# One more chunk turned by TensorE instead of by DMA in a fused retention and gated feed-forward kernel, with the state copies, the loads' lead and two casts moved along with it

## The chip, the cores and the metric

The kernel runs on one core of one Trainium2 chip. A core has a matrix engine (TensorE, PE in the profile, with its weight loads as PEld), a vector engine (VectorE, DVE), a scalar engine (ScalarE, ACT), a general engine (GpSimd, POOL) and a sync engine (SyncE, SP), which here issues nearly all DMA transfers. Each engine works through its own queue in order; semaphores tie the queues together. The metric is the device time of one execution in microseconds (us), the median of several runs.

## The reference

First comes a retention layer: attention without a softmax, with a decay per head. For 8 batches, 8 heads, 576 positions and a head dimension of 64:

```python
scores = scale * np.matmul(q, k.transpose(0, 1, 3, 2))
gamma = 1.0 - 2.0 ** (-5.0 - np.arange(H))
Dmat = np.where(rel >= 0, gamma[:, None, None] ** rel[None, :, :], 0.0)   # rel = i - j
attn_out = np.matmul(scores * Dmat, v)
```

Its result, laid out as 4608 tokens of 512 numbers, is `x` for a gated layer with 1536 hidden units:

```python
gate = 1.0 / (1.0 + np.exp(-(x @ w_gate)))
out = (gate * (x @ w_val)) @ w_out
```

## The kernel before

**Chunks.** The decay is folded into q and k by two tables of powers, one for each position in a chunk. Retention then runs over chunks of 128 positions: scores inside a chunk, masked to a triangle, times v, plus q times a running state, the sum of all earlier k-v products of the batch. Batch 0's first 512 positions and batch 1's first 256 are done at the start, in pairs. The other 30 chunks are the list `STEPS`, numbered from 0: 0 and 1 are the end of batch 1, 2 to 5 the four full chunks of batch 2, 6 is the 64 last positions of batches 0 and 1 together, 7 to 10 the full chunks of batch 3, 11 the last positions of batches 2 and 3, and so on.

**What a chunk passes through.** SP loads its k, q and v (`load`, L163, or in halves L166 for a chunk of last positions). `casts_to` has k and q multiplied by their tables and rounded to bf16 (`cast_qk`, L398: on POOL, q of the first two chunks on DVE), has v cast (`cast_v`, L403), and from chunk 2 on calls `cross` (L407): a DMA transpose on SP's queue that turns k and q so that the head dimension lies on the partitions. Chunks 0 and 1 are turned on TensorE instead, by `turn_step`: eight transposing matmuls (L589) into the two PSUM banks `pv` and `tr`, which ACT and DVE copy to SBUF (L591). The turned copy, tile T, is read by the scores (`scores`, L628) and by the products of q with the state (`inter`, L670). The same two banks later hold the chunk's values (`intra`, L654).

`casts_to(x)` also sets the loads' lead: before chunk x's casts it queues the loads up to chunk x + 1, from chunk 12 on up to x + 2. `next_slot(s)` does the scores of chunk s and the values of chunk s - 1, then calls `casts_to(s + 3)`; `next_two` does two chunks at once. Both put what is left over (copies of values, state sums, their bf16 copies) into a list `pending`, of which one entry is taken after each later unit of work.

**The feed-forward layer.** Its tokens go in blocks: 512 tokens at the start, then `BLOCKS`: 256 tokens from row 512 (number 0), 256 from row 768 (number 1), and seven of 512 from row 1024 on (2 to 8). Blocks 0 and 1 are plain: 12 units of hidden products (`h_units`, L847: gates to ACT's sigmoid, L850, values to DVE's product, L852) and 6 units of output products (`op_units`, L1174). Blocks of 512 use a scheme of seven products instead of eight, for which sums of quarters of the weights, of x and of the hidden units are made. The order of their units is written out by hand (`ORDER`): `g16` is product 6 of the gates' second third, `w07` product 7 of the first third of the values, `v8` a plain value product. In `ORDER`, marks behind a colon place sums of the hidden units on DVE or POOL (L902 and L908, tile gsum), which the output products (L1072) read. POOL also does some of the gate-times-value products of these blocks (L989).

**Order around the change.** The main loop over `BLOCKS` goes unit by unit. After each unit it may emit a sum of weights that is due (`weight_sums`, L312 and L338), the in-place sums that `PLACES` puts after that unit, in block 2 the casts that `CASTS_AT` puts there, one pending entry, or the next slot. Blocks 0 and 1 hold four and two slots (chunks 0 to 3, 4 and 5), and block 1 also the first double slot: after its second output unit come the values of chunk 5 and the scores of chunks 6 and 7. Values of later chunks follow in block 2.

`first_batch_state` assembles the state that the last positions of batch 0 (chunk 6) need, in a tile `sf`, by two DVE copies and two small DMAs on SP's queue (L796); it is called in slot 3.

Of the kernel before, what the change touches and what calls it, by code (L numbers as in the profile page):

```python
# [16 lines left out]
def kernel(  # L17
# [139 lines left out]
    def load(s):  # L157
        b, c = STEPS[s]
        tiles = []
        for nm, src in (("k", k), ("q", q), ("v", v)):  # L160
            t = landing([P, H, D], f"{nm}32_{s}", s >= 8)
            if c < LAST:
                nc.sync.dma_start(out=t, in_=src[b, :, c * P:(c + 1) * P, :].rearrange("h p d -> p h d"))  # L163
            else:
                for j, (bj, tj) in enumerate(pieces_of(s)):
                    nc.sync.dma_start(out=t[half(j)], in_=src[bj, :, tj:tj + 64, :].rearrange("h p d -> p h d"))  # L166
            tiles.append(t)
        loaded[s] = tiles
# [137 lines left out]
    def wo_sums(i, part, parts, eng=nc.vector):  # L306

        fp = slice(part * (NFC // 2) // parts, (part + 1) * (NFC // 2) // parts)
        b11, b12, b21, b22 = (wo_sb[:, r::2, c:c + DM // 2][:, fp] for r in range(2) for c in (0, DM // 2))
        t1, t2, t4 = (wt_sb[:, j, fp] for j in range(3))  # L310
        to, a, b = ((t1, b12, b11), (t2, b22, t1), (b12, b22, b12), (t4, b21, t2))[i]
        eng.tensor_tensor(out=to, in0=a, in1=b, op=ALU.subtract)  # L312
# [80 lines left out]
    def cast_qk(s, i, eng):  # L393
        c = STEPS[s][1]
        if i == 1:
            natural_qk[s] = nat_pool.tile([P, 2, M, P], BF16, tag="qk", name=f"qk_{s}")
        tab = (qtab, ktab)[i][:, c, :].rearrange("p (y m) -> p y m", y=2).unsqueeze(3).to_broadcast([P, 2, M, D])
        eng.tensor_tensor(out=natural_qk[s][:, i].rearrange("p m (y d) -> p y m d", y=2),  # L398
                          in0=by_halves(loaded[s][1 - i]), in1=tab, op=ALU.mult)

    def cast_v(s, eng):
        natural["v", s] = nat_pool.tile([P, H, D], BF16, tag="v", name=f"v_{s}", bufs=6)
        eng(out=natural["v", s], in_=loaded[s][2])  # L403

    def cross(s):
        t = att_pool.tile([P, 2, M, P], BF16, tag="T", name=f"T_{s}", bufs=6)
        nc.sync.dma_start_transpose(out=t.rearrange("p j m t -> p (j m) t"),  # L407
                                    in_=natural_qk[s].rearrange("p j m d -> p (j m d)"))
        turned[s] = t
# [168 lines left out]
            cols = slice(t0, t0 + P)  # L578
            eng(out=x_out(slice(i * k, (i + 1) * k), cols), in_=x_in(ps[:, at_m:at_m + k], cols))

    TURNED = 2

    def turn_step(s):

        t = att_pool.tile([P, 2, M, P], BF16, tag="T", name=f"T_{s}", bufs=6)
        for i, ((pool, tag), eng) in enumerate(zip(VALS, (on_act, on_dve))):
            ps = pool.tile([P, M, P], BF16, tag=tag, name=f"turn_{s}_{i}")
            for m in range(M):
                nc.tensor.matmul(ps[:, m, :], lhsT=natural_qk[s][:, i, m, :], rhs=ident, is_transpose=True,  # L589
                                 start=(m == 0), stop=(m == M - 1))  # L590
            eng(out=t[:, i], in_=ps)  # L591
        turned[s] = t
# [81 lines left out]
    def slot(s):  # L674

        if s > 0:
            val_ps[s - 1] = values(M + 2, s - 1)
            intra(s - 1)
            inter(s - 1, [(0, 1), (0, 1)], apart=True)
        scores(s)  # L680
        if STEPS[s][1] < LAST:
            products(s)
        mask(s)
# [84 lines left out]
    def after(s, i):  # L768

        makes = STEPS[s][1] < LAST  # L770
        to_bf16 = on_act if s < 6 else on_pool
        if i == 0:
            if s > 0:
                leave_share(s - 1, 0)
                leave_share(s - 1, 1)
            if makes:
                add_state(s, 0)
        else:
            if s > 0:
                leave_other(s - 1, i - 1)  # L780
                leave_own(s - 1, 2 - i)
                if i == 2 and dealt(cols_of(s - 1, 0)):
                    x_sums(at_col[s - 1], nc.vector)
            if i == 1 and makes:
                add_state(s, 1)
            if makes and (s, i - 1) in totals:
                b, c = STEPS[s]
                keep_state((b, c, i - 1), totals.pop((s, i - 1)), to_bf16)


    def first_batch_state():

        whole = new_state((0, LAST - 1, NJ - 1))
        for hh in range(2):
            for y in range(2):
                (nc.vector.tensor_copy if hh == y else nc.sync.dma_start)(  # L796
                    out=whole[half(y), hh::2, :], in_=sbd[3][half(hh), 2 * y:2 * y + 2, half(hh)])
        state[0, LAST - 1, NJ - 1] = whole

    pending = []  # L800

    done = {"ld": 0, "cast": 0}

    def loads_to(s):
        while done["ld"] <= min(NS - 1, s):
            load(done["ld"])
            done["ld"] += 1

    def casts_to(s):
        while done["cast"] <= min(NS - 1, s):  # L810
            x = done["cast"]
            loads_to(x + (1 if x < 12 else 2))
            cast_qk(x, 1, nc.gpsimd)
            cast_qk(x, 0, nc.vector if x < 2 else nc.gpsimd)
            if x >= TURNED:
                cross(x)
            cast_v(x, on_dve if x == 0 else on_pool)
            done["cast"] += 1

    def next_slot(s):  # L820
        slot(s)
        if s == 3:
            first_batch_state()
        casts_to(s + LEAD_CAST)
        for i in range(3):
            pending.append(lambda i=i: after(s, i))
        if s + 1 == 1:
            pending.insert(2, lambda: turn_step(s + 1))
# [98 lines left out]
    def quarter_units(gvs, t0):  # L927
# [82 lines left out]
        def value(fc):  # L1010
# [3 lines left out]
            for kc in range(NKC):  # L1014
# [6 lines left out]
        return quarter, value  # L1021

    EARLY = ((10, "g01"), (13, "g05"), (13, "g02"))
    PLACES = (((1, 0), "g", 0), ((1, 1), "g", 1), ((1, 2), "w", 0), ((2, 0), "o", 0), ((2, 1), "w", 1),
              ((2, 9), "o", 1), ((2, 12), "g", 2), ((2, 45), "o", 2))
    CASTS_AT = (5, 32)
    SECOND = 7
    ORDER = ("g06 g11 w05 g03 w01 g15 g16 g12 g07 w06 g13 g21 g17 w03 w11 w07 g04 w02 g14 w04 w16:0t"
             " g26:00 w12 w15:01 w17:02 g25 g22 w13 g27 g23 w14:10 v8 v9:1t:2a g24 v10:11 v11:12:2b").split()
# [420 lines left out]
    SPARE = {}  # L1450
    for at, kind, u in PLACES:
        SPARE.setdefault(at, []).append((lambda u=u: wo_sums(2, u, 3)) if kind == "o" else (lambda kind=kind, u=u: w_sums(kind, 2, u, nc.vector)))
# [4 lines left out]
    for w, (t0, n) in enumerate(BLOCKS):  # L1457
        nxt = BLOCKS[w + 1] if w + 1 < len(BLOCKS) else None
        last = last_step(nxt[0] + nxt[1]) if nxt else NS - 1
        end = slots + (SINGLE[w] if w < len(SINGLE) else 0)  # L1460
        begin = slots
        total = 2 * NFC * 4 * n + 12 * 512 * (n // P)
        n_h = NFC if n <= 256 else 2 * NFC
        if n == 512:
            n_h = len(steps_of(t0))
        n_twos = 0
        gone = 0
        twos = []
        at = end
        while not twos and valued + (end - begin) < last or twos and twos[-1][0][-1] < last:  # L1470
            vals = list(range((twos[-1][0][-1] if twos else valued + end - begin) + 1, at))
            twos.append((vals, list(range(at, min(at + 2, NS)))))
            at = min(at + 2, NS)
        if w < 1:
            twos = []

        for i, cols in enumerate(ffn_units(t0, n, nxt)):
            if w < 2 and i % 2 == 1 and weight_sums:
                weight_sums.pop(0)()
            if w == 2 and i in CASTS_AT:  # L1480
                casts_to(done["cast"])
            for x in SPARE.get((w, i - n_h if w == 1 else i), ()):
                x()
            gone += cols
            pieces += 1
            if stores and (nxt is None or w + 2 == len(BLOCKS) and pieces % 4 == 0):
                leave()
            if n > 256 and i % 2 and i < n_h:
                continue
            if pending:  # L1490
                pending.pop(0)()
            elif slots < end and gone * (end - begin) >= (slots - begin) * (total - 5 * 2048):
                next_slot(slots)
                valued = slots - 1
                slots += 1
            elif twos and i - n_h >= (SECOND if n == 512 and len(twos) == 1 else 1):
                next_two(*twos[0], n == 512, not n_twos, len(twos) == 1)
                n_twos += 1
                valued = twos[0][0][-1]
                slots = max([slots] + [s + 1 for s in twos.pop(0)[1]])  # L1500
        assert not twos and slots >= end
        while pending:
            pending.pop(0)()
# [31 lines left out]
```

## Time and profile before

| | |
|---|---|
| timed runs, median (lowest to highest of 3) | 314.72 us (313.76 to 315.41) |
| the profiled execution, whole | 312.58 us |
| its span, first to last instruction | 310.9 us |
| mean granted clock of TensorE | 0.994 |
| busy: PE / DVE / POOL / ACT | 300.3 / 232.8 / 202.5 / 193.6 us |
| moved by DMA | 55.24 MB, mean 178 GB/s |
| DMA transposes | 28, of 2.7 to 6.0 us from issue to landing, median 3.9 |
| the double slot in block 1 | from 84.67 us |
| the first block of 512 from row 1024 | from 93.02 us |

Times inside the execution are counted from the start of the span. A line of a timeline gives the start, the time taken, the engine, the line of the kernel, the operation and its tiles (written <- read), shapes, a count, and in brackets the idle time before it with what ended that. In a group of waits the figures are the sum, the count and the longest, in us. The slices of the page are 40 equal parts of the span, a digit for each: the busy share in tenths, or for PEclk the granted clock in tenths of full speed.

### The profile page before, as it was taken

To read this page: it belongs to the slowest core of one execution; us is meant where nothing else is said; L and a number is where in the kernel's file an instruction comes from. 1 tells how busy PE (TensorE), PEld (TensorE's weight loads), DVE (VectorE), ACT (ScalarE), POOL (GpSimd) and SP (SyncE) were. 2 spreads that over 40 slices of the span, in tenths; PEclk is the share of its full clock that TensorE was granted. 3 is DMA by queue.
4 is the path that set the end of the run, shared out by engine and by line. 5 is a ranking of instruction groups with operands and counts; after the bars stand their busy time and mean duration, and the time that the engine had idled before them with its cause. 6 is when DMAs were issued, how large, how long until landed. Compare 5 with 4: busy or idle time off the path is not lost. (4 is left out here: it accounts for less than half of the span.)

```text
span 310.9 us, 10391 instructions
## 1 busy us (share of the span) xinstructions
PE 300.3 (97%) x4262; PEld 236.2 (76%) x4278; DVE 232.8 (75%) x492; ACT 193.6 (62%) x424; POOL 202.5 (65%) x240
## 2 busy tenths in 40 slices
PE   8999999999979999999999999999999999999994
PEld 7664456868738878887888788878887888788773
DVE  6857967886874997699769876987699769835943
ACT  6855454545329736973797379736973797359730
POOL 6784555643743799878787877797779707810780
PEclk9999999999979999999999999999999999999999
DMA  7999999997999658995479659957981183003004
GB/s 217 345 373 392 350 271 237 223 177 171 203 208 223 149 124 155 247 249 147 112 170 249 156 130 191 243 120 128 183 207 65 36 271 104 2 21 118 3 1 136
DMA packets 146048, 55.24 MB, mean 178 GB/s; under 512 B 125392, under 2 KB 137936, under 8 KB 146000
## 3 DMA queue, kind: packets, MB, share of 16 engines
q1 hardware_dynamic: 145200, 53.92, 71.1%
q8 instruction: 33, 0.54, 0.7%
q10 hardware_dynamic: 800, 0.66, 0.7%
q14 instruction: 15, 0.12, 0.1%
HBM read 37.75 MB, written 9.44 MB: 152 GB/s over the span
## 5 line engine op out<-in xcount | busy, mean ns | idle before, releaser
L398 POOL TENSOR_TENSOR qk<-k,ktab 128x512 bf16<-128x512 f32 x30 | 32.2, 1073 | 22.7 <-DMA k<-in_k_dram 18.7
L966 PEld LDWEIGHTS <-wg_sb 128*128 128x128 bf16 x336 | 32.9, 98 | 5.5
L989 POOL TENSOR_TENSOR gv<-gv,wu 128x512 bf16<-128x512 bf16 x14 | 16.3, 1165 | 29.8 <-DVE wu L1001 29.8
L1072 PEld LDWEIGHTS <-gsum 128*128 128x128 bf16 x336 | 32.3, 98 | 4.3 <-POOL gsum L908 0.4
L398 POOL TENSOR_TENSOR qk<-q,qtab 128x512 bf16<-128x512 f32 x28 | 30.8, 1100 | 1.5 <-DMA q<-in_q_dram 1.5
L902 POOL TENSOR_TENSOR gsum<-gv 128x512 bf16<-128x512 bf16 (+1 forms) x28 | 27.0, 965 | 5.6 <-DVE gv L989 4.7
L966 PEld LDWEIGHTS <-wgt_sb 128*128 128x128 bf16 x252 | 24.6, 98 | 3.3
L643 DVE TENSOR_TENSOR pt<-row,tri 128x256 bf16<-128x256 f32 x60 | 21.6, 416 | 6.6 <-PE row L636 5.0
L1072 PEld LDWEIGHTS <-gv 128*128 128x128 bf16 x240 | 23.0, 98 | 4.3
L1015 PE MATMUL h<-xT,wv_sb 128*128 128x512 bf16 x105 | 24.9, 379 | 0.4
L966 PE MATMUL gatea<-xsum,wg_sb 128*128 128x256 bf16 x168 | 25.2, 273 | 0.0
L1001 DVE TENSOR_TENSOR gu<-gatee,gu 128x512 f32<-128x512 f32 x21 | 14.4, 688 | 12.6 <-ACT gateg L993 6.3
L966 PEld LDWEIGHTS <-wv_sb 128*128 128x128 bf16 x224 | 21.9, 98 | 2.5
L989 POOL TENSOR_TENSOR gv<-gv,ws 128x512 bf16<-128x512 bf16 x14 | 17.1, 1221 | 7.6 <-DVE ws L1004 7.6
L1004 DVE TENSOR_TENSOR gs<-gatea,gs 128x512 f32<-128x512 f32 x21 | 14.4, 688 | 10.1 <-PE gatea L966 9.3
L712 ACT CAST xT<-val 128x256 bf16<-128x256 f32 x50 | 15.7, 386 | 9.1 <-PE val L670 6.0
L403 POOL CAST v<-v 128x512 bf16<-128x512 f32 x29 | 19.4, 670 | 1.4 <-DMA v<-in_v_dram 1.4
L1018 DVE TENSOR_TENSOR gv<-gv,h 128x512 bf16<-128x512 bf16 x28 | 18.4, 679 | 2.4 <-PE h L1015 2.4
L1015 PEld LDWEIGHTS <-wv_sb 128*128 128x128 bf16 x112 | 11.0, 98 | 10.2
L987 ACT ACTIVATE gv<-gs 128x512 bf16<-128x512 f32 x21 | 13.4, 639 | 7.6 <-DVE gs L1004 7.6
L966 PEld LDWEIGHTS <-wvt 128*128 128x128 bf16 x168 | 16.4, 98 | 2.2 <-issue 0.3
L604 ACT CAST sb<-s 128x256 bf16<-128x256 f32 x46 | 17.4, 420 | 1.1 <-DVE s L763 0.2
(178 smaller groups left out, 826.4 us busy)
## 6 DMA issues: line engine op xcount, KB each, us to landing
k<-in_k_dram SPq DMA_DIRECT2D x26, 256.0 KB, 3.8
q<-in_q_dram SPq DMA_DIRECT2D x26, 256.0 KB, 4.3
v<-in_v_dram SPq DMA_DIRECT2D x26, 256.0 KB, 4.7
out_dram<-ob SPq DMA_DIRECT2D x25, 256.0 KB, 3.0
wg<-in_moe_w_gate_dram SPq DMA_DIRECT2D x12, 256.0 KB, 5.3
wv<-in_moe_w_val_dram SPq DMA_DIRECT2D x12, 256.0 KB, 5.2
wo<-in_moe_w_out_dram SPq DMA_DIRECT2D x12, 256.0 KB, 5.0
v32p<-in_v_dram SPq DMA_DIRECT2D x6, 256.0 KB, 4.9
```

What stands on the lines that cost most here:

```text
L398: eng.tensor_tensor(out=natural_qk[s][:, i].rearrange("p m (y d) -> p y m d", y=2), in0=by_halves(loaded[s][1 - i]), in1=tab, op=ALU.mult)
L403: eng(out=natural["v", s], in_=loaded[s][2])
L604: eng(out=state[key], in_=src)
L643: nc.vector.tensor_tensor(out=probs[s][:, y], in0=row_ps[s][y][:, 0], in1=tri.unsqueeze(1).to_broadcast([P, M, 64]), op=ALU.mult)
L712: nc.scalar.copy(out=x_out(ALL, cols_of(s, i)), in_=x_in(val_ps[s][i], cols_of(s, i)))
L902: nc.gpsimd.tensor_tensor(out=s3, in0=a11, in1=a21, op=ALU.subtract)
L966: nc.tensor.matmul(ps[:, f], lhsT=w[:, kc, f * P:(f + 1) * P], rhs=x[:, kc], start=(first and f == 0 and kc == 0), stop=(f == 1 and kc == ...
L989: eng.tensor_tensor(out=to, in0=to, in1=src, op=ALU.mult)
L1001: nc.vector.tensor_tensor(out=me["u2"], in0=e, in1=me["u2"], op=ALU.add)
L1015: nc.tensor.matmul(ps, lhsT=wv_sb[:, kc, fc * P:(fc + 1) * P], rhs=xT(kc, slice(t0, t0 + 512)), start=(kc == 0), stop=(kc == NKC - 1))
L1018: nc.vector.tensor_tensor(out=gvs[fc], in0=gvs[fc], in1=ps, op=ALU.mult)
L1072: nc.tensor.matmul(ps[:, b], lhsT=left(fp)[:, b * P:(b + 1) * P], rhs=right(fp), start=(first and fp == 0 and b == 0), stop=(fp == NFC // ...
```

## The change

Six edits:

- `TURNED` becomes the set of chunks that TensorE turns: 0, 1 and now 7. Chunk 7's DMA transpose is no longer issued.
- `turn_step(7)` is emitted in block 1 after its last hidden unit (`n_h + TURN_AT` is 11) and so ahead of its first output unit.
- `first_batch_state` is called in slot 1 instead of slot 3.
- The loads' lead is given by chunk in `AHEAD`: 2 for chunk 0, 1 for chunks 1 to 8, 2 for chunk 9, 1 for chunk 10, 0 for chunk 11, and 2 as before from chunk 12 on. Before, it was 1 for all chunks up to 11.
- The casts of chunks 10 and 11 in block 2 are emitted after units 2 and 12 instead of 5 and 32.
- The eight in-place sums of weights in `PLACES` stand in other places: two in block 1 (units 12 and 15) instead of three, and six in block 2 (units 0, 6, 7, 10, 17, 43) instead of five (0, 1, 9, 12, 45).

```diff
-    TURNED = 2
+    TURNED = (0, 1, 7)
...
+    AHEAD = (2, 1, 1, 1, 1, 1, 1, 1, 1, 2, 1, 0)
...
-            loads_to(x + (1 if x < 12 else 2))
+            loads_to(x + (AHEAD[x] if x < len(AHEAD) else 2))
             cast_qk(x, 1, nc.gpsimd)
             cast_qk(x, 0, nc.vector if x < 2 else nc.gpsimd)
-            if x >= TURNED:
+            if x not in TURNED:
                 cross(x)
...
-        if s == 3:
+        if s == 1:
             first_batch_state()
...
-    PLACES = (((1, 0), "g", 0), ((1, 1), "g", 1), ((1, 2), "w", 0), ((2, 0), "o", 0), ((2, 1), "w", 1),
-              ((2, 9), "o", 1), ((2, 12), "g", 2), ((2, 45), "o", 2))
-    CASTS_AT = (5, 32)
+    PLACES = (((1, 0), "w", 0), ((1, 3), "g", 1), ((2, 0), "g", 0), ((2, 6), "o", 2), ((2, 7), "o", 0),
+              ((2, 10), "g", 2), ((2, 17), "w", 1), ((2, 43), "o", 1))
+    TURN_AT = -1
+    CASTS_AT = (2, 12)
...
+            if w == 1 and i == n_h + TURN_AT:
+                turn_step(7)
```

## The prediction

> **What bounds the kernel now.** I read the busy row first, then TensorE's waits, then the stretch that they point to in slices of 1 us, then the timelines of the queues that end there. TensorE (PE) is busy in 300.3 of the span's 310.9 us, so only its idle time, its slow time and work given to it can move the end. The page's slices have one hole after the start, the 12th and 13th of 40, and the granted clock falls there; the waits name it.
>
> ```profile
> PE 300.3 (97%) x4262; PEld 236.2 (76%) x4278; DVE 232.8 (75%) x492; ACT 193.6 (62%) x424; POOL 202.5 (65%) x240
> PE   8999999999979999999999999999999999999994
> PEclk9999999999979999999999999999999999999999
> PE row L628 <- DMA T<-qk: 2.3, 1, 2.3
> ```
>
> By the microsecond (busy us of PE, PEld, DVE, ACT, POOL; granted clock; DMA share; GB/s):
>
> ```profile
> 84.00:85.00 1.00, 1.00 (x44) 0.46 (x42) 1.00 (x2) 0.00 (x0) 0.71 (x2) 1.00 2.55 155
> 85.00:86.00 1.00, 0.18 (x24) 0.07 (x10) 1.00 (x4) 0.00 (x0) 0.67 (x1) 1.00 0.22 7
> 86.00:87.00 1.00, 0.00 (x0) 0.00 (x0) 0.75 (x4) 0.00 (x0) 0.00 (x0) 1.00 0.71 156
> 87.00:88.00 1.00, 0.51 (x40) 0.51 (x42) 0.08 (x1) 0.00 (x0) 0.00 (x0) 1.00 1.28 279
> 88.00:89.00 1.00, 0.90 (x3) 0.34 (x3) 1.00 (x4) 0.00 (x0) 0.12 (x1) 0.71 1.03 234
> 89.00:90.00 1.00, 1.00 (x4) 0.38 (x3) 0.77 (x3) 0.69 (x2) 1.00 (x2) 0.50 1.42 259
> 90.00:91.00 1.00, 1.00 (x4) 0.37 (x3) 0.52 (x1) 1.00 (x4) 1.00 (x2) 0.50 0.95 172
> 91.00:92.00 1.00, 1.00 (x4) 0.36 (x3) 1.00 (x3) 0.05 (x1) 0.67 (x1) 0.59 0.85 194
> ```
>
> See two losses in a row: PE stands until 87.43, and then runs at half clock. The timeline says why: chunk 7's scores wait for its turned copy, whose DMA left SP only at 81.38, behind chunk 8's loads (its casts were done at 80.44).
>
> ```profile
> 80.34 0.86 SPq L163 DMA_DIRECT2D v<-in_v_dram  x1
> 81.38 2.32 SPq L407 DMA_TRANSPOSE T<-qk  x1
> 82.85 1.89 PE L1174 MATMUL op<-wo_sb,gv 128*128 128x512 bf16 x7
> 83.73 1.14 DVE L312 TENSOR_TENSOR wt_sb<-wo_sb,wt_sb 128x512 bf16<-128x512 bf16 x1
> 84.67 0.32 PE L654 MATMUL val<-pt,v 64*64 64x64 bf16 x16
> 87.43 0.32 PE L628 MATMUL row<-T 64*64 64x64 bf16 x16 [2.25 <-DMA T<-qk]
> 88.10 5.09 PE L1174 MATMUL op<-wo_sb,gv 128*128 128x512 bf16 x15 [0.16 <-issue]
> ```
>
> That DMA took 6.0 us to land, the longest of 28 (median 3.9). From 93 us on PE has no wait above 0.4 us: what it gains before reaches the end if the engines that feed it keep up.
>
> **The change, part by part.** Sums are against the profiled execution: span 310.9, 312.58 us in all. The three timed runs have a median of 314.72, so I add 2.14 to bring a forecast onto their scale. 0.5% of it, 1.57 us, is about what a measurement can tell from no change.
>
> *Chunk 7 turned on PE.* Gone: the wait, 2.25 us, as long as nothing else is late there. Added on PE: eight transposes. The same step for chunk 1 started at 54.99 and the next matmul at 55.44: **+0.45**. They come where PE reached 82.85, and their input was cast by 80.44. ACT copies one half (579 to 586 ns); it is idle for 6.53 us there, cost nothing, else 0.6. DVE copies the other half (415 to 425 ns) behind two of its own: the gate product (to 83.81) and L312, which took 1.14 instead of 0.41 while POOL cast chunk 8's q (to 84.59). So the copy ends at 84.87 + 0.42 = 85.29. Both copies must be over before chunk 5's values (L654) may write the same two PSUM banks; PE comes there at 82.85 + 0.45 + 1.82 = 85.12. With some 0.1 to be signalled, **+0.25**; bounds 0 (L312 at 0.41) and 1.25 (L312 held until chunk 8's v cast ends at 85.67: 85.95 + 0.42). I take the value of the row. Next on DVE are one sum of weights (0.42 to 0.58) and the two glance copies (0.21) that the second half of chunk 5's state products waits for. They end near 86.1, PE arrives near 85.95: **+0.15** (0 to 0.4). Before, the long wait covered both.
>
> *The half clock.* From 88 to 92 the slices lose 0.29 + 0.50 + 0.50 + 0.41 = 1.70 us. The waits of 0.41 at 62.00 and 0.42 at 66.46 left the clock at 1.00, so I take the 2.25 us for the cause and the whole as gained: **-1.70**; bounds -1.70 and 0. The sum takes this from the rows alone. [...]
>
> *SP's queue.* With the transpose gone, chunk 9's load is issued at about 81.2 instead of 83.74, then come the transposes of 8, the loads of 10 and (lead 2 at chunk 9) 11, and the transpose of 9, with the out stores after it. Chunk 8's transpose still waits for its casts (84.59). The load of 11 would start near 88.8 and, at its 4.6 us for six issues, be out at 93.4, its last v landed near 96. The scores of 8 and 9 are at 113, so their later place costs nothing. Lead 2 at chunk 0 moves no issue past another: nothing else is on SP between. Lead 0 at chunk 11 puts load 12 behind the transpose of 11 with loads 13 and 14; those land near 106, and chunk 12 was cast at 118.55. Nothing either way; without that cover a load would cost its 3.6 to 4.7 us of landing.
>
> *State copies from slot 3 to slot 1.* Two DMAs (0.61 + 0.63 of issue) go from in front of load 7 to in front of load 5. That puts load 5, the transposes of 4 and 5 and load 6 up to 1.28 later: T of chunk 4 landed at 68.6 and was used at 72.08, of 5 at 74.65 against 78.08. Margins above 3.4, nothing. Two DVE copies (0.19 + 0.38) come before 59.96, where DVE idled 0.45 us, but slot 2's values at 62.00 waited for DVE already: **+0.10** (0 to 0.59).
>
> *Casts of 10 and 11 (units 5, 32 to 2, 12).* POOL did chunk 11's three casts from 108.89 to 111.67, in front of the sums that the output products wait for. PE's sixth product took 1.61 us to the next instead of 1.31, since the last sum it reads ended at 117.15:
>
> ```profile
> 116.48 0.67 POOL L908 TENSOR_TENSOR gsum<-gsum,gv 128x256 bf16<-128x256 bf16 x1
> 117.44 1.47 PE L1072 MATMUL qe<-wt_sb,gsum 128*128 128x256 bf16 x12
> ```
>
> At unit 12 they fall into POOL's 5.77 us of idleness before 101.64. The sums come 2.8 us sooner in POOL's queue, on top of all else being 3 us sooner: **-0.30** (0 if PE's lead eats it).
>
> *Weight sums on DVE.* The block before ends with two instead of three, the next has six instead of five, 0.42 each. Four of them fall into DVE's idle 2.94 and 1.09 us before 98.48; the one at unit 17 adds 0.42 where DVE idles 0.18 and 0.26 by 103.40. Nothing; else 0.4.
>
> Sum: -2.25 + 0.45 + 0.25 + 0.15 - 1.70 + 0.10 - 0.30 = **-3.30**. That is 309.3 on the profiled scale and **311.4** against the median.
>
> **The rivals.** *Half clock stays* (0.13). [...] Against it: the clock fell at once after the only long wait. -3.30 + 1.70 = -1.60: 313.1, on the edge of 0.5%.
>
> *The wait moves to DVE's copy* (0.06). For it: L312 stood for POOL, and chunk 8's v cast follows at once. Then values wait 1.25 instead of 0.25, -2.3; if that halves the clock too, -0.6: 314.1. Against it: L312 got in between the two casts before.
>
> *Slower: chunk 11's casts block POOL* (0.09). POOL works in order. In front of its gate products, first needed at 101.64 - 3.3 = 98.3, now stand casts that need load 11. DVE's sums at 104.01 follow POOL's end at 103.95, and DVE has no idle time from 104.6 to 119: POOL late is PE late. If load 11 gets out no sooner than it did (from 95.18, last issue 99.77, 3.1 to land: 102.9), the last cast ends at 103.6, 5.3 late: +2.0, 316.7. It starts to cost when v lands after about 97.6 and eats all from 100.9. Against it: SP has one transpose less and that load stands one transpose sooner.
>
> *Given back* (0.04): PE arrives sooner at feeders that don't, and nothing is left: 314.7. POOL was 92 to 100% busy from 110 to 131 but the casts leave it 2.8 us; nothing else waits.
>
> **How the numbers follow.** The forecast has 0.68. Its own bounds: all costs at their low end -3.8, all at their high end (0.8 of the copy's 1.25, as the rest is a rival) -1.3, which gives 310.9 to 313.4; the runs scatter by 0.7 to 1.0 around their median, so its own range is 310.0 to 313.4. The range reaches over the half clock to the copy's wait: 310.0 to 314.6, and leaves out the slower rival and part of "given back". Faster by over 0.5% (under 313.15): 0.66 of the forecast, 0.07 of the half clock, 0.03 of the copy: 0.76. Slower (over 316.3): the slower rival and 0.01 of the rest: 0.10. Within: 0.14.
>
> **What would show it.** Right: no wait of row on a T at chunk 7; granted clock 1.00 from 85 to 95; eight more transposes near 83 and 27 DMA transposes; values of chunk 5 begin by 85.5; the block of 512 from row 1024 begins near 89.8 instead of 93.02; POOL casts chunk 11 before its first gate product, and no gap in the sixth output product. Wrong: a clock of 0.5 near 88 all the same, a DVE copy ending after 86, or POOL idle before a cast of chunk 11 later than 98.

## The result and the profile after

Over 20 runs each, the median is 309.94 us with the change (308.24 to 311.31) and 312.35 us before (309.3 to 315.95): 2.41 us less. The ratio of the comparison is 0.9951, with a 95% interval from 0.9929 to 0.9973. It is nearer to 1 than the ratio of the medians (0.9923) because the comparison leaves out runs more than 1.5% above their kernel's fastest, which are six of the 20 of before and none after; in the later sets of before, where each run has its clock, the 14 that it leaves out are all at 0.988 to 0.993, so it leaves out a part of what the change takes away. By that ratio the gain is 1.5 us. The forecast time was 311.4 us in a range of 310.0 to 314.6: the new median lies 0.06 below it, because the three runs that the forecast stood on (314.72) were high for a kernel whose median over 20 is 312.35. The profiled execution took 309.39 us, 3.19 less than the 312.58 of the one before; the forecast was 3.30 less.

Of the changed kernel, the busy row and the slices of the page, where the hole in PE and the dip of the clock were:

```profile
span 307.7 us, 10424 instructions
PE 299.9 (97%) x4286; PEld 235.6 (77%) x4286; DVE 233.3 (76%) x493; ACT 194.4 (63%) x425; POOL 202.4 (66%) x240
PE   8899999999999999999999999999999999999994
PEclk9999999999999999999999999999999999999999
```

The hole and the dip are gone, and no scores wait for a T any more. The timeline of the changed kernel at chunk 7 (start, time taken, what):

```profile
82.92 0.68 PE L589 MATMUL turn<-ident,qk 128*128 128x128 bf16 x8
83.34 0.59 ACT L591 COPY T<-turn 128x512 bf16<-128x512 bf16 x1 [0.50 <-PE turn L589]
83.43 1.89 PE L1176 MATMUL op<-wo_sb,gv 128*128 128x512 bf16 x8
83.79 0.82 DVE L312 TENSOR_TENSOR wt_sb<-wo_sb,wt_sb 128x512 bf16<-128x512 bf16 x1
84.53 0.41 DVE L591 COPY T<-turn 128x512 bf16<-128x512 bf16 x1
85.25 0.32 PE L654 MATMUL val<-pt,v 64*64 64x64 bf16 x16
85.46 0.49 PE L628 MATMUL row<-T 64*64 64x64 bf16 x32
86.17 3.63 PE L1176 MATMUL op<-wo_sb,gv 128*128 128x512 bf16 x16
```

The scores of chunks 6 and 7 now run as one group of 32, and the output products behind them begin at 86.17 (before: 88.10) and take 3.63 us for 16 matmuls (before: 5.09 for 15). The block from row 1024 begins at 89.63 instead of 93.02, 3.39 us sooner, and the end comes 3.2 us sooner: what was gained before 90 us reached the end but for 0.2. That is a balance: 0.3 more was won at the sixth output product (below), and 0.75 was lost in a wait that neither profile of before shows.

```profile
148.02 0.22 PE L670 MATMUL val<-T,sb 64*64 64x64 bf16 x3 [0.75 <-issue]
```

It was 0.67 us with the turn alone, 0.78 in the kernel before with its wait filled (below) and 0.36 in the changed kernel's second profile. The profile doesn't name what ended it, and its cause stays open.

So one profiled execution on each side gives the forecast, and the medians give three quarters of it. Why is the question of half of the experiments.

### The profile page after: what moved, and what is told of

Its sections match the earlier page's. It is cut to its first block, busy times and chain, and to the rows that moved or that the text cites. A ratio compares the mean times of both kernels' runs of the same rounds, so it can differ in the third digit from the quotient of the medians.

```text
span 307.7 us, 10424 instructions
## 1 busy us (share of the span) xinstructions
PE 299.9 (97%) x4286; PEld 235.6 (77%) x4286; DVE 233.3 (76%) x493; ACT 194.4 (63%) x425; POOL 202.4 (66%) x240
## 5 line engine op out<-in xcount | busy, mean ns | idle before, releaser
L1016 PE MATMUL h<-xT,wv_sb 128*128 128x512 bf16 x112 | 26.5, 379 | 0.0
```

The costliest lines, as they stand in the source:

```text
L1016: nc.tensor.matmul(ps, lhsT=wv_sb[:, kc, fc * P:(fc + 1) * P], rhs=xT(kc, slice(t0, t0 + 512)), start=(kc == 0), stop=(kc == NKC - 1))
```

## The experiments

A base to read them by: in four sets, 102 executions of the kernel before that have a clock with them fall into two groups. 56 have a mean granted clock of 0.988 to 0.995 and take 313.9 us in the mean (311.8 to 316.9); 46 have 0.997 to 1.000 and take 311.2 (309.5 to 313.5). Half clock for 3.4 us, the length of the dip in the first profile of before, lowers the mean clock of a span of 311 us by 0.0055, so I take the first group for the executions with the dip. All 32 executions of the changed kernel have 0.996 or more; what they lack to 1.000 need not lie at chunk 7: in the second profile of the changed kernel (0.996) the clock was 1.00 in every microsecond from 82 to 96.

**The turn alone.** On the kernel before:

```diff
-    TURNED = 2
+    TURNED = (0, 1, 7)
-            if x >= TURNED:
+            if x not in TURNED:
+            if w == 1 and i == n_h - 1:
+                turn_step(7)
```

> The kernel before with chunk 7 turned on TensorE at the same place as in the change, and nothing else of it. Theory (the wait for chunk 7's transpose and the half clock behind it are the gain): no wait of the scores for a T at chunk 7, clock 1.00 from 85 to 95 us, first block of 512 at about 89.8 us instead of 93.02, nearly the whole gain of the change, -2.0 to -3.0 us against the kernel before; the wait for POOL's sums in the sixth output product stays or grows from 0.3 us, because chunk 11's casts still stand in front of them. Rival (the moves around the turn carry the gain): within 0.5 us of the kernel before.

Measured: median 309.80 us, against 313.15 for the kernel before on the same chip; ratio 0.9925 (0.9894 to 0.9956). No wait for a T at chunk 7, block from row 1024 at 89.42, all nine executions at a clock of 0.997 or more. The sixth output product still took 1.61 us to the next (112.22 to 113.83): the wait for POOL's sums stayed as it was and didn't grow. The 3.35 us between the medians are more than the 2.0 to 3.0 expected; against a second set of before on the same chip (312.0, below) they are 2.2. The turn alone is the whole gain that can be measured; the rival falls.

**All but the turn.** On the changed kernel, chunk 7 goes back to the DMA:

```diff
-    TURNED = (0, 1, 7)
+    TURNED = (0, 1)
-            if w == 1 and i == n_h + TURN_AT:
-                turn_step(7)
```

> The changed kernel with chunk 7 turned by the DMA again; state copies, loads' lead, casts and weight sums stay moved. Theory: TensorE waits for chunk 7's transpose again, 1.5 to 2.5 us, the clock halves for about 3.4 us behind it, and the time is that of the kernel before, within 0.6 us. Rival (the moves alone carry the gain): 2 us or more below the kernel before.

Measured: median 312.22 us against the same 313.15; ratio 0.9949 (0.9907 to 0.9991). In the profile the wait is back (2.40 us) with the half clock behind it, and 7 of 12 executions have a clock of 0.994 or less. At 0.93 below, it missed the "within 0.6" by little; the shares of half clock (7 of 12, and 21 of 32 for the kernel before) leave part of that to the draw. The ratio is as low as that of the change itself (0.9951), so by groups: the seven at half clock take 313.8 us in the mean, as in the kernel before on this chip (313.7), and the five others 310.3 against 311.6 there. Whether the moves are worth a microsecond at full clock, five executions can't tell, and with the turn in place they are worth nothing (below). They do not take away the wait or the dip, and all 12 have a mean of 312.3 us where the changed kernel has 310.0.

```profile
PE row L628 <- DMA T<-qk: 2.4, 1, 2.4
```

**The wait filled with work.** On the kernel before, ten matmuls of zeros before chunk 7's scores, in their bank:

```diff
-            scores(s, banks)
+            scores(s, banks, 10 if s == 7 else 0)
...
+        for _ in range(busy):
+            nc.tensor.matmul(row_ps[s][0].rearrange("p a m t -> p (a m) t"), lhsT=blank,
+                             rhs=blank[:, 0:64].unsqueeze(1).to_broadcast([P, 2 * M, 64]), start=True, stop=True)
```

> The kernel before with ten matmuls of zeros (512 columns each, 2.16 us) put between the scores of chunk 6 and those of chunk 7, written to a bank that the scores then overwrite. TensorE computes in the time in which it waited. Theory (the wait causes the half clock): the same place in time for chunk 7's scores, 87.1 to 87.5 us, but the clock stays at 1.00 and the end comes 1.7 us sooner wherever the kernel before has its half clock. Rival (the half clock comes by itself, or TensorE is at half rate in any case there): half clock near 88 us all the same, time as before or slower.

Measured: none of 12 executions at half clock (0.997 and more). The profiled span was 309.2 us, 1.7 below the 310.9 of before, as expected. Chunk 7's scores began at 86.52, not at 87.1 to 87.5, as this profile reached chunk 5's values 0.9 us sooner (83.73 against 84.67). The timeline shows the zeros in place of the wait:

```profile
84.18 2.33 PE L626 MATMUL row<-blank 128*128 128x512 bf16 x10
86.52 0.32 PE L631 MATMUL row<-T 64*64 64x64 bf16 x16
86.96 1.25 PE L1177 MATMUL op<-wo_sb,gv 128*128 128x512 bf16 x5
```

So here the clock fell for the idle wait and not for the place or the time: the zeros took the executions at half clock from 21 of 32 (the kernel before on this chip) to none of 12. But the median over all executions, 312.66 against 313.15, ratio 1.0004 (0.9972 to 1.0035), is no gain. The mean of the 12 is 312.6 us: 1.2 less than that of the executions with the dip on this chip (313.7; expected 1.7 less), 1.0 more than that of the others (311.6). That the zeros cost time where the wait would have been shorter than they are (2.33 us in this profile) is my reading; no profile of before with a shorter wait was taken.

**The kernel before once more**, unchanged.

> The kernel before, unchanged, for another profiled execution and the spread of its times. Theory (the spread of 309.3 to 316.0 us is that of the wait at chunk 7 and of the half clock, which depend on when the DMA lands): wait at chunk 7 between 0 and 4 us, and executions of a lower mean clock are the longer ones, about 1 us for each 0.3% of clock and more for the wait itself. Rival (the spread lies elsewhere): the same wait of 2.3 us in every profile and no tie between clock and time.

Measured: median 312.0 us; 5 of 12 executions at half clock. By the microsecond, this profile (columns as before: stretch, PE, PEld, DVE, ACT, POOL, granted clock, DMA share, GB/s):

```profile
85.00:86.00 1.00, 0.20 (x28) 0.09 (x12) 1.00 (x3) 0.00 (x0) 0.41 (x1) 1.00 0.03 3
86.00:87.00 1.00, 0.00 (x0) 0.00 (x0) 0.82 (x5) 0.00 (x0) 0.34 (x1) 1.00 0.79 174
87.00:88.00 1.00, 0.34 (x40) 0.35 (x40) 0.00 (x0) 0.00 (x0) 0.27 (x1) 1.00 1.27 278
88.00:89.00 1.00, 1.00 (x27) 0.49 (x14) 0.85 (x3) 0.00 (x0) 0.00 (x0) 1.00 1.10 247
89.00:90.00 1.00, 1.00 (x6) 0.46 (x5) 0.97 (x3) 0.83 (x3) 0.91 (x1) 1.00 1.11 252
```

The wait is as long as in the first profile (2.45 us against 2.25), and yet the clock stays at 1.00. The span is 309.5 instead of 310.9. Clock and time are tied, against the rival: the five with the dip take 313.6 us in the mean, the seven others 311.1. The theory's wait "between 0 and 4" is met, but it is not the wait's length that sets these two profiles apart. The same wait costs 1.70 us of half clock in one execution and nothing in the next.

**Pauses of three lengths.** On the changed kernel, ACT repeats its copy of chunk 7's turned half, 5, 7 or 10 times in all, so that TensorE waits there:

```diff
-            eng(out=t[:, i], in_=ps)
+            for _ in range(5 if s == 7 and i == 0 else 1):
+                eng(out=t[:, i], in_=ps)
```

Their base is the changed kernel again:

> The changed kernel, unchanged, as the base for the three pauses that follow. All executions at a clock of 0.996 or more, within 0.5 us of 309.9 us.

It gave a median of 310.23 us, all 12 executions at 0.996 or more.

> The changed kernel with ACT's copy of chunk 7's turned half done five times instead of once, so that chunk 5's values wait. A copy of this kind follows the last in about 0.5 us, so the values start near 86.0 instead of 85.25: a pause of TensorE of some 0.75 us. [...] Rival (any pause there halves the clock): 2 us and more later.

> The same with seven copies: a pause of some 1.75 us. [...] Rival (the clock falls with a fixed chance whenever TensorE waits over a microsecond): about 6 in 10 at half clock, two groups of times 2 us apart.

> The same with ten copies: a pause of some 3.25 us, longer than the wait of the kernel before. [...] Rival (half clock has nothing to do with the length): 6 in 10 or fewer.

The pauses came out longer than planned, since a copy follows the last in about 0.6 us (five took 3.06). The wait rows of the three profiles:

```profile
PE val L655 <- ACT T L592: 1.2, 1, 1.2
```

```profile
PE val L655 <- ACT T L592: 2.4, 1, 2.4
```

```profile
PE val L655 <- ACT T L592: 4.3, 1, 4.3
```

| pause in the profile | executions at half clock | median, us | above the base |
|---|---|---|---|
| none (changed kernel) | 0 of 32 | 309.94, 310.23 | |
| 1.15 us | 0 of 12 | 310.83 | 0.60 |
| 2.25, 2.45 us (kernel before) | 56 of 102 | | |
| 2.43 us | 4 of 12 | 313.37 | 3.14 |
| 4.28 us | 6 of 6 | 316.56 | 6.33 |

Half clock came with length here, not with a fixed chance for any wait: in none of 12 executions at 1.15 us, in part of them near 2.4, in all six at 4.28. The rival of the first run falls; that of the third (6 in 10 or fewer; up to then the kernel before had 26 of 44) would give six of six about once in twenty sets; the second run can't tell, as its pause (2.43 us) was as long as the wait of the kernel before. At ten copies the mean was 6.0 us above the base. Its profile shows why a long pause costs more than one dip: the pause runs from 86.73 to 91.01, the clock falls at 89.22, 2.5 us into it, and is back at 96.06, after 6.8 us, twice the 3.4 of the first profile of before.

```profile
89.00:90.00 1.00, 0.00 (x0) 0.00 (x0) 0.00 (x0) 0.94 (x3) 1.00 (x2) 0.61 1.07 164
96.00:97.00 1.00, 1.00 (x6) 0.49 (x5) 1.00 (x3) 0.00 (x0) 0.71 (x2) 0.97 1.02 229
```

At the shortest pause, 1.15 us, the price is no more than the pause itself: 0.60 us between the medians.

**The other moves taken back**, each on the changed kernel. Casts and lead:

```diff
-    AHEAD = (2, 1, 1, 1, 1, 1, 1, 1, 1, 2, 1, 0)
+    AHEAD = (1,) * 12
-    CASTS_AT = (2, 12)
+    CASTS_AT = (5, 32)
```

> The changed kernel with the casts of chunks 10 and 11 back after units 5 and 32 and the loads' lead back at 1 up to chunk 11. Theory: nothing changes up to the first block of 512; the sixth output product of that block waits 0.3 us again for POOL's sums, and the end is 0.3 us later than the changed kernel at most, within the scatter of its times (309.9 to 310.2 us in two sets). Rival (the casts carry part of the gain): 1 us or more later.

Measured: 310.21 us, none of 12 executions at half clock. The sixth output product (113.35) took 1.60 us to the next (114.95), where the changed kernel's (112.47) took 1.31. The 0.3 us is there in the profile and too small for the medians.

State copies back to slot 3, and `PLACES` as before:

```diff
-        if s == 1:
+        if s == 3:
             first_batch_state()
-    PLACES = (((1, 0), "w", 0), ((1, 3), "g", 1), ((2, 0), "g", 0), ((2, 6), "o", 2), ((2, 7), "o", 0),
-              ((2, 10), "g", 2), ((2, 17), "w", 1), ((2, 43), "o", 1))
+    PLACES = (((1, 0), "g", 0), ((1, 1), "g", 1), ((1, 2), "w", 0), ((2, 0), "o", 0), ((2, 1), "w", 1),
+              ((2, 9), "o", 1), ((2, 12), "g", 2), ((2, 45), "o", 2))
```

> The changed kernel with the state copies back in slot 3 and the in-place sums of weights back in their old places. Theory: within 0.3 us of the changed kernel; two sums of weights instead of one now stand on DVE between the turned half's copy and the glance copies, which may add 0.4 us before the second half of chunk 5's state products. Rival (these two moves carry part of the gain): 1 us or more later.

Measured: 309.97 us, none of 12 executions at half clock. These moves are worth nothing that can be measured.

The lead alone, with the casts left early:

```diff
-    AHEAD = (2, 1, 1, 1, 1, 1, 1, 1, 1, 2, 1, 0)
+    AHEAD = (1,) * 12
```

> The changed kernel with the loads' lead back at 1 up to chunk 11, the casts left at units 2 and 12. Chunk 11's load then goes out behind the transpose of chunk 9 and the out stores, near 92.5 instead of 90 us, and its last v lands near 100. Theory (POOL works in order, and in the changed kernel its first gate product starts right behind chunk 11's casts): POOL's first gate product is 1.5 to 3 us late and TensorE waits by most of that in the block from row 1024, so 1 to 2.5 us later than the changed kernel. Rival (slack behind POOL takes it up): within 0.5 us of the changed kernel.

Measured: 312.19 us (310.83 to 316.07), 2.0 to 2.2 us above the two kernels before, which ran on the same chip, and three of 12 executions at a clock of 0.995, the upper edge of the group with the dip (where it fell in them was not profiled). The nine others take 312.2 us in the mean, so the loss is not that of the clock alone. The gain is nearly gone: ratio to the kernel before 1.0016 (0.9973 to 1.0059). First POOL in the changed kernel, then in this one:

```profile
95.45 1.04 POOL L398 TENSOR_TENSOR qk<-k,ktab 128x512 bf16<-128x512 f32 x1 [1.38 <-DMA k<-in_k_dram]
97.56 0.61 POOL L403 CAST v<-v 128x512 bf16<-128x512 f32 x1
98.25 1.28 POOL L990 TENSOR_TENSOR gv<-gv,wu 128x512 bf16<-128x512 bf16 x1
```

```profile
97.88 1.04 POOL L398 TENSOR_TENSOR qk<-k,ktab 128x512 bf16<-128x512 f32 x1 [3.61 <-PE gatea L967]
100.50 0.61 POOL L403 CAST v<-v 128x512 bf16<-128x512 f32 x1 [0.18 <-PE gatea L967]
101.06 1.16 POOL L990 TENSOR_TENSOR gv<-gv,wu 128x512 bf16<-128x512 bf16 x1
```

Chunk 11's load is issued from 93.44 instead of 89.97, so its casts end late and POOL's first gate product starts at 101.06 instead of 98.25. (The bracket of the first cast names a matmul; but the two halves of k were issued from 93.44 to 95.27, and in the kernel before the second half of chunk 11's k took 3.7 us to land, so I take the load for what the cast stood for.) From the block's first matmul (90.54 and 89.63) that is 1.9 us late. In the profile TensorE then waits where it did not before:

```profile
105.75 0.60 PE L967 MATMUL wa<-xsum,wv_sb 128*128 128x256 bf16 x4 [0.58 <-DVE ws L1005]
```

The profiled execution (311.18 us) is one of this kernel's shorter ones, and half of the 1.8 us between its span and the changed kernel's lies before the block (90.54 against 89.63). What the longer ones lose beyond 0.58 us was not profiled. All three changed entries of `AHEAD` go back in this run; the trace points to chunk 9's, which places chunk 11's load. Casts moved ahead without the lead cost 2 us in the medians; the lead is what makes that move harmless.

## Why the prediction was right, and where its sizes were off

- **The wait at chunk 7, -2.25.** Right. It is gone, and the turn alone does it.
- **Transposes, +0.45.** 0.51 (82.92 to 83.43).
- **Waits for DVE's copy, +0.25, and for the glance copies, +0.15.** Neither came. The copy was over at 84.94, not 85.29, because L312 took 0.82 instead of 1.14. The values began at 85.25, when TensorE got there, and the state products went on without a wait. The 0.1 for the signal was my estimate; in the three runs with pauses, where the values did wait for a copy, they began 0.05 to 0.06 us after ACT's last copy had ended (87.33 to 87.38 at five copies).
- **Half clock, -1.70.** The cause was right (none of 12 executions at half clock with the wait filled), though of the two short waits held against it the one at 66.46 is a row of the weight loads (PEld; TensorE was busy for 0.95 us of that microsecond). Its weight was off: this is the term that separates forecast and medians. It was priced from one execution as if every execution had it. 56 of 102 have it. An execution of before with the dip takes 313.9 us in the mean, one without 311.2: against the changed kernel's medians of 309.9 and 310.2 the change is worth some 3.8 us to the first kind and 1.1 to the second. I argue, but have not shown, that the 2.7 between the kinds is more than 1.70 because longer waits bring the dip more often. Two things on record bear on it. Under the pause of seven copies, whose length ACT sets and not a DMA, the four executions with the dip take 314.5 us in the mean and the eight others 312.8, just 1.70 apart, though these few scatter by over 3 us. And nine of the 56 have a clock of 0.988 or 0.989, like the profile with 6.8 us at half clock, and take 315.9 us, the other 47 313.6: a second stretch at half clock is a part of it, if that is what these nine had.
- **The rival that half clock stays (0.13).** It fell: the clock is 1.00 from 85 to 95 us in the profile after, and none of the 32 executions of the changed kernel has a mean under 0.996. What was held against it, that the clock fell at once, was put too short: it fell at 88.4, 1.0 us after the wait had ended (88 to 89 has a mean of 0.71), and in the pause of 4.28 us it fell 2.5 us into it. Behind the wait of 2.45 us it stayed at 1.00. What sets the moment, no run shows.
- **SP's queue.** Chunk 9's load went out at 81.72 (forecast 81.2), chunk 11's from 89.97 (88.8). Its last v, issued at 94.3, needed at least 3.1 us to land (the shortest of its group), so it was there no sooner than 97.4 and not near 96, close to the 97.6 from which the forecast saw a cost. The last cast ended at 98.17, and POOL's first gate product followed at 98.25, forecast need 98.3. Of the slack that I put at over a microsecond 0.1 us was left.
- **The slower rival.** It didn't happen, but its mechanism is real: with the lead taken back, POOL's first gate product was 1.9 us late and the median rose by 2.0. Of the forecast's two reasons against it, one transpose less on SP and the load of chunk 11 a place sooner, the first alone was not enough; the load had to stand ahead of chunk 9's transpose and the out stores.
- **Casts, -0.30.** Right in the profile: 1.61 us became 1.31, and 1.60 with the casts taken back. Not measurable in the medians.
- **State copies, +0.10, weight sums, 0.** Slot 2's values waited 0.20 us instead of 0.41, for ACT's copy in both profiles and not for DVE, as the forecast read it; and the kernel with both taken back is as fast.
- **The base.** Three runs of before, with a median of 314.72, were taken for its level; over 20 it is 312.35. With over six microseconds between its fastest and slowest execution, three runs can't place it. From 312.35 the same sum would have given 309.05, 0.9 below the 309.94: that the forecast time came within 1.5 us is in part luck, as the gain taken too large made up for some of the base taken too high.

## What to carry to other kernels

When one engine is busy nearly all the time, look for the few waits that it has and for what the clock does behind them: here a wait of 2.25 us cost 3.95 us in the profiled execution, and one of 1.15 us no more than itself. Before a price is taken from one profile, ask whether every execution pays it; a mean clock beside each run's time answers that. A cast that is moved ahead in an engine's queue can end up standing for its load: here the casts moved ahead without the lead cost 2.0 us in the medians. So move cast and load together.

## What the runs showed of the hardware

Executions at half clock, by the length of the wait in the profile: 0 of 12 at 1.15 us, 4 of 12 at 2.43, 56 of 102 for the kernel before (2.25 and 2.45 us in two profiles), 6 of 6 at 4.28. The dip lasted 3.4 us at 0.50 in the first profile of before, and 6.8 us in the profile with the pause of 4.28 us, where it began 2.5 us into the pause. A wait of 2.25 us had it and one of 2.45 us had not, in two executions of the same kernel. With ten matmuls of zeros (2.33 us) in place of the wait, the mean clock was 0.997 or more in 12 of 12 executions.
